# The same attention and MLP kernel with its instructions put in another order: lengths in the planner changed, ranks of runs of operations shifted

## The chip, the core and the metric

The kernel runs on one core of a Trainium2 chip. The metric is device time in microseconds, the median of several executions. The engines are TensorE (PE, matmuls; its weight loads are shown as PEld), VectorE (DVE), ScalarE (ACT), GpSimd (POOL) and SyncE (SP, which here issues DMAs). Each takes its own instructions strictly in the order in which they were written.

## The reference

A chunk-selecting attention over 4 batches, 8 heads, 768 tokens, 64 dimensions, and then an MLP over all 3072 tokens (512 to 2048 to 512, with ELU):

```python
k_min = np.min(k_chunks, axis=3)
k_max = np.max(k_chunks, axis=3)
ub = np.sum(np.maximum(q * k_min, q * k_max), axis=-1)
ub = np.where(causal, ub, -1000000000.0)
top_chunks = np.argsort(ub, axis=-1)[..., -top_k:]
scores = scale * np.matmul(q, k.transpose(0, 1, 3, 2))
mask = sel & (pos[:, None] >= pos[None, :])
...
attn = attn / (np.sum(attn, axis=-1, keepdims=True) + 1e-09)
return np.matmul(attn, v).astype(np.float32)
...
h = x @ w_in
g = np.where(h > 0.0, h, alpha * (np.exp(np.minimum(h, 0.0)) - 1.0))
return (g @ w_out).astype(np.float32)
```

Keys come in 24 chunks of 32. For each query and chunk an upper bound of the score is computed from the chunk's smallest and largest key values; the 6 best causal chunks are kept. Scores outside them and above the diagonal are masked.

## The kernel before

**Tiling.** Two heads make a pair, so a batch has 4 pairs and the whole problem 16. A pair's 768 queries are done in two halves of 384. Two pairs make a quad, for which chunk selection is done together. The MLP is done for a batch's half (384 tokens) at a time.

**The stages of a pair.** Loads of q, k and v (`stage`, `vd`; L396, L437; in the first batch `gT`, L475, L481), issued by SP. In batch 0 (`first_prep`) fp32 matmuls turn q and k (L498), ACT copies k in bf16 with a strided pattern (L508), POOL casts q (L548) and v (L539). In the other batches (`pair_prep`) DVE transposes k and q (L409, L427) and reduces k's chunks to minimum and maximum (L413), and POOL casts two heads of k, two of q, and v (L548, L440). `quad_sel` computes the chunk bounds (PE, L580), their six best (DVE, L597 to L620), and puts the mask rows into `rhs` (POOL, L631). `pair_attend` does scores (PE, L672), exponentials (ACT, L699), the diagonal (POOL, L718), the product with values (PE, L731), the division (DVE, L744, L747), and a transpose to `xT` (PE L756, ACT L759).

**The MLP.** `mlp` computes 16 up projections of 4 matmuls (L781) into `psH` (into `psS` in the last batch), the exponential (ACT, L791), the rest of ELU into `gT` (ACT L796, DVE L799, or DVE L820 and L825; L809 and L814 in the last batch), and for each of 3 token tiles 4 parts of 4 down projections (L838) into `psM` (`psMT` in the last batch), evicted by ACT (L846) and stored by SP (L850). An MLP operation can run as soon as its batch's `xT` is there, so the MLP of one batch is interleaved with the attention of the next.

**The order.** Nothing is emitted directly. Every step is registered with `add(engine, length, rank, emit, ...)` in a planner (`Plan`), with what it reads, writes, and which buffers it takes and frees. `Plan.order` then plays the engines through: repeatedly it takes, for each engine, the operation that can start first by the planned lengths; among those ready when the engine is free, the one with the lowest rank `prio` goes first. The engine whose choice starts earliest is served. Operations are emitted in this sequence, and that is the order of each engine's instructions on the chip. The ranks are positions in units of one pair: `pos(u, hf)` for attention, `mpos(b, hf)` for the MLP, less a lead for loads and preparation. Lengths are formulas, `act(n)` for ACT, `dve(n)` for DVE, and for POOL casts `0.13 + 0.00096 * n`. The plan treats POOL and those DVE operations marked `port` as exclusive of each other.

Of the kernel before, what the change touches and what calls it, by code (L numbers as in the profile page):

```python
# [17 lines left out]
S = 768  # L18
# [10 lines left out]
HALF = S // 2  # L29
# [22 lines left out]
LATER = {4: 0}  # L52
RATES = (232.0, 232.0, -1.4, 0.75)
MERGE = (False, False, False, True)

DUMP = None

# [6 lines left out]
class Plan:  # L64
# [17 lines left out]
    def add(self, eng, dur, prio, emit, reads=(), writes=(), alloc=(), free=(), lat=None, tag="",  # L82
# [33 lines left out]
        self.ops.append(o)  # L116
        return o

    def order(self):
        ops = self.ops  # L120
        for o in ops:
            o.left = len(o.deps) + len(o.after)
            o.ready = 0.0
            o.start = o.end = None
            for d in o.deps:
                d.users.append(o)
            for d in o.after:
                d.followers.append(o)
        free_slots = {c: [(0.0, i) for i in range(n)] for c, n in self.caps.items()}
        held = {}  # L130
        engines = {}
        waiting = {}
        for o in ops:
            waiting.setdefault(o.eng, [])
            engines[o.eng] = self.BEGIN
            if not o.left:
                waiting[o.eng].append(o)
        n_left = len(ops)
        port = {"POOL": 0.0, "DVE": 0.0}
        out = []  # L140
        while n_left:
            best = None
            for e, t in engines.items():
                cand = None
                for o in waiting[e]:
                    r = max(t, o.ready)
                    if o.port and o.eng in port:
                        r = max(r, port["DVE" if o.eng == "POOL" else "POOL"])
                    ok = True
                    for h in o.alloc:  # L150
                        fs = free_slots[h[0]]
                        if not fs:
                            ok = False
                            break
                        r = max(r, min(fs)[0])
                    if not ok:
                        continue
                    key = (r, o.prio, o.n) if r > t else (t, o.prio, o.n)
                    if cand is None or key < cand[0]:
                        cand = (key, o, r)  # L160
                if cand is not None and (best is None or cand[2] < best[2]):
                    best = cand
            assert best is not None, "no operation can start"
            _, o, r = best
            slots = []
            for h in o.alloc:
                fs = free_slots[h[0]]
                s = min(x for x in fs if x[0] <= r)
                fs.remove(s)
                held[h] = s[1]  # L170
                slots.append((h, s[1]))
            o.start = r
            o.end = r + o.dur
            engines[o.eng] = o.end
            if o.port and o.eng in port:
                port[o.eng] = o.end
            waiting[o.eng].remove(o)
            for h in o.free:
                free_slots[h[0]].append((o.end + o.lat, held[h]))
            for u in o.users:  # L180
                u.left -= 1
                lag = 0.0 if u.eng == o.eng and o.eng in ("PE",) else o.lat
                u.ready = max(u.ready, o.end + lag)
                if not u.left:
                    waiting[u.eng].append(u)
            for u in o.followers:
                u.left -= 1
                u.ready = max(u.ready, o.start)
                if not u.left:
                    waiting[u.eng].append(u)  # L190
            out.append((o, slots))
            n_left -= 1
        return out
# [3 lines left out]
def kernel(  # L197
# [88 lines left out]
    add = plan.add  # L286
# [99 lines left out]
    def pair_prep(u):  # L386

        kb, qb, vx, km = new("kb", "qb", "vx", "km")
        PAIR[u] = dict(kb=kb, qb=qb, vx=vx, km=km)

        def load(h, src):
            def f():
                for hd in range(2):
                    for e in range(2):
                        r0 = 64 * hd + 32 * e
                        nc.sync.dma_start(out=tiles[h][r0:r0 + 32, :].rearrange("c (m i) -> c m i", i=32),  # L396
                                          in_=src[2 * u + hd, e])
            return f

        kd, qd, kt, qt, qa, kx, vd = new("stage", "stage", "kt", "qt", "qa", "kx", "vd")  # L400
        pa = pos(u, 0)
        pl = pa - 4.0
        pr = pa - AHEAD
        for i in range(2):
            PAIR[u]["qt", i], PAIR[u]["qa", i] = qt, qa
        late = [("asked", LATER[u])] if u in LATER else []
        fetch(2.0, 393.0, 128.0, pl, load(kd, ke), [kd], alloc=[kd], reads=late)
        fetch(2.0, 393.0, 128.0, pl + 0.2, load(qd, qe), [qd], alloc=[qd], reads=late)
        add("DVE", dve(S), pr, lambda: nc.vector.transpose(out=tiles[kt], in_=tiles[kd]),  # L409
            reads=[kd], writes=[kt], alloc=[kt], free=[kd])  # L410
        for x, op in ((0, AOT.min), (1, AOT.max)):
            add("DVE", dve(S), pr,
                lambda x=x, op=op: nc.vector.tensor_reduce(  # L413
                    out=tiles[kx] if x else tiles[km][:, 0, 0:NCH],
                    in_=tiles[kt].rearrange("p (c w) -> p c w", w=CHUNK),
                    axis=mybir.AxisListType.X, op=op),
                reads=[kt, "kept"], writes=[kx] if x else [(km, 0, i) for i in range(2)],
                alloc=[kx] if x else [km])
        add("POOL", 0.16, pr,
            lambda: nc.gpsimd.tensor_tensor(out=tiles[km][:, 1, 0:NCH], in0=tiles[kx], in1=tiles[km][:, 0, 0:NCH],  # L420
                                            op=AOT.subtract),
            reads=[kx] + [(km, 0, i) for i in range(2)], writes=[(km, 1, i) for i in range(2)], free=[kx])
        for hd in range(2):
            cast(pr + 0.2, S, lambda hd=hd: (tiles[kb][0:64, hd, :], tiles[kt][64 * hd:64 * hd + 64, :]),
                 reads=[kt], writes=[(kb, i, hd) for i in range(2)], alloc=[] if hd else [kb],
                 free=[kt] if hd else [])
        add("DVE", dve(S), pr + 0.1, lambda: nc.vector.transpose(out=tiles[qt], in_=tiles[qd]),  # L427
            reads=[qd], writes=[qt], alloc=[qt], free=[qd])
        add("ACT", act(S - SEL0), pr + 0.1,
            lambda: nc.scalar.activation(out=tiles[qa], in_=tiles[qt][:, SEL0:S], func=AF.Relu),  # L430
            reads=[qt], writes=[qa], alloc=[qa])
        for hd in range(2):
            cast(pr + 0.2, S, lambda hd=hd: (tiles[qb][0:64, hd, :], tiles[qt][64 * hd:64 * hd + 64, :]),
                 reads=[qt], writes=[(qb, i, hd) for i in range(2)], alloc=[] if hd else [qb])

        def vload():
            nc.sync.dma_start(out=tiles[vd], in_=v3[:, 12 * u:12 * u + 12, :])  # L437
        fetch(0.5, 393.0, 205.0, pl + 1.2, vload, [vd], alloc=[vd], reads=late)
        add("POOL", 0.13 + 0.00096 * S, pr + 1.0,
            lambda: nc.gpsimd.tensor_copy(out=tiles[vx][:, :, 0:D], in_=tiles[vd]),  # L440
            reads=[vd, "ones"], writes=[(vx, i) for i in range(2)], alloc=[vx], free=[vd])

    def first_prep(u, hf):
# [60 lines left out]
            return x.rearrange("q (j p) -> q p j", j=4)  # L504
        add("PE", TURN, pr, turn(bk, at_k), reads=[(hk, i0), "ident"], writes=[bk[0]], alloc=bk, free=fk)
        for hd in range(2):
            add("ACT", act(HALF), pr,
                lambda hd=hd: nc.scalar.activation(  # L508
                    out=tiles[kb][0:64, hd, a:b].rearrange("q (p j) -> q p j", j=4),
                    in_=tok(ps(bk, None, None)[64 * hd:64 * hd + 64, :]), func=AF.Copy),  # L510
                reads=[bk[0]], writes=[(kb, hf, hd), (bk[0], "turn")], alloc=[] if hf or hd else [kb])
# [23 lines left out]
        for hd in range(2):  # L535
            cast(pr + 0.2, HALF, lambda hd=hd: (tiles[qb][0:64, hd, a:b], tiles[qt][64 * hd:64 * hd + 64, a:b]),
                 reads=[qt], writes=[(qb, hf, hd)], alloc=[] if hf or hd else [qb])
        add("POOL", 0.13 + 0.00096 * HALF, pr + 1.0,
            lambda: nc.gpsimd.tensor_copy(  # L539
                out=tiles[vx].rearrange("p (h n) d -> p h n d", h=2)[:, :, 3 * hf:3 * hf + 3, 0:D],  # L540
                in_=tiles[sv][:, iv].rearrange("p (h n d) -> p h n d", h=2, d=D)),
# [3 lines left out]
    def cast(pr, w, what, **kw):  # L545
        def f():
            o, i = what()
            nc.gpsimd.tensor_copy(out=o, in_=i)  # L548
        add("POOL", 0.13 + 0.00096 * w, pr, f, **kw)

    def quad_sel(g, hf):

# [210 lines left out]
    def mlp(b, hf):  # L763
        tail = b == B - 1
        if True:
# [64 lines left out]
            for tt in range(3):  # L830
                bm = bank("MT" if tail else "M")
                for part in range(4):
                    pr = mpos(b, hf) + 2 + 2 * (4 * tt + part) / 12

                    def down(bm=bm, tt=tt, part=part, gt=gt):
# [2 lines left out]
                            nc.tensor.matmul(pm, lhsT=tiles[gt][:, fc, 128 * tt:128 * tt + 128],  # L838
                                             rhs=w_out_sb[:, fc, :], start=(fc == 0), stop=(fc == NFC - 1))
                    add("PE", 4 * 0.2165, pr, down,  # L840
                        reads=[("w_out", part)] + [(gt, fc) for fc in range(4 * part, 4 * part + 4)],
                        writes=[(bm[0], part)], alloc=bm if part == 0 else [],
                        free=[gt] if tt == 2 and part == 3 else [])
                osb, = new("osb")
# [92 lines left out]
```

## Time and profile before

| what | value |
|---|---|
| median of 3 runs | 280.38 us (280.21 to 285.49) |
| span of the profiled execution, first to last instruction | 278.4 us |
| median less span | 2.0 us |
| bytes moved by DMA | 29.82 MB |
| DVE, ACT, POOL busy | 73%, 72%, 46% of the span |

A time for the profiled execution that includes what lies around its span is not given; the median of the runs stands in for it. Busy time of PE includes each matmul's pipeline latency up to its modelled end, so a busy PE is not PE at its peak. In groups, the first number after the bar is busy time in us, the next the mean of one instruction in ns, and after the second bar stands idle time of the engine ahead of those instructions with what ended it. In the waits, the three numbers are the total in us, the number of waits, and the longest. The chain of waits follows the work that ended last back to what released it; in order of time its rows have start, length and what ran.

### The profile page before, as it was taken

The page shows a single profiled execution, that of the slowest core. Times are in us where ns is not written, and L with a number is a line of the kernel's source. Part 1 is how long each engine was busy: PE and PEld are TensorE (multiplying, and loading weights), DVE is VectorE, ACT ScalarE, POOL GpSimd, SP SyncE. Part 2 cuts the span into 40 slices and gives each one's busy share as a digit, 9 for nine tenths or more (in the row PEclk, how much of TensorE's full clock was granted, in tenths as well). Part 3 has the DMA queues.
Part 4 walks back from the last instruction along what each step waited for, and adds up shares of the span by engine and source line. Part 5 has one row for each costly group of instructions (what it writes and reads, how often), then busy time and mean ns, then how long its engine had stood idle before and what let it go on. Part 6 is the DMA issues. An engine that isn't in the chain of part 4 may idle for free.

```text
span 278.4 us, 7242 instructions
## 1 busy us (share of the span) xinstructions
PE 266.7 (96%) x2732; PEld 164.0 (59%) x2732; DVE 204.2 (73%) x546; ACT 201.4 (72%) x381; POOL 128.0 (46%) x235
## 2 busy tenths in 40 slices
PE   7989899989999999999999999999999999999994
PEld 7968566644565556655665656565565556555541
DVE  6876965799999989999989588657856434767610
ACT  2879899946699697999899958685868564544311
POOL 5668863356797797966965625102320201000000
PEclk9999999999999999999999999999999999999999
DMA  7999999988998599999497101101101111101122
GB/s 187 232 211 188 197 203 207 146 131 163 189 171 156 73 143 201 165 163 170 87 164 114 38 2 38 40 0 40 39 4 38 40 39 40 38 0 40 38 75 75
DMA packets 111330, 29.82 MB, mean 107 GB/s; under 512 B 101056, under 2 KB 108224, under 8 KB 111296
## 3 DMA queue, kind: packets, MB, share of 16 engines
q1 hardware_dynamic: 106656, 24.78, 48.4%
q0 software_dynamic: 4224, 4.19, 9.2%
q8 instruction: 21, 0.34, 0.6%
q10 hardware_dynamic: 416, 0.39, 0.5%
q14 instruction: 13, 0.11, 0.1%
HBM read 27.26 MB, written 6.29 MB: 121 GB/s over the span
## 4 chain that ended last, share of the span: by engine, by line
PE 68%; ACT 15%; DVE 6%; DMA 4%; issue 3%; SPq 1%; POOL 0%; ACTq 0%; DVEq 0%
PE psM L838 20%; PE psH L781 15%; PE psS L781 7%; PE psMT L838 7%; PE psS L672 7%; ACT pt L699 7%; PE psO L731 5%; ACT e L791 3%; PE psS L580 3%; DMA gT<-in_v_dram 2%; DMA gT<-in_k_dram 2%; ACT psH L796 1%; ACT xT L759 1%; DVE gT L799 1%; PE psT L756 1%
## 5 line engine op out<-in xcount | busy, mean ns | idle before, releaser
L699 ACT ACTIVATE pt<-psS 128x768 bf16<-128x768 f32 (+1 forms) x120 | 91.5, 799 | 4.1 <-PE psS L672 2.6
L781 PE MATMUL psH<-xT,w_in_sb 128*128 128x384 bf16 x384 | 75.2, 325 | 1.6 <-ACT xT L759 0.9
L838 PE MATMUL psM<-w_out_sb,gT 128*128 128x512 bf16 x288 | 72.5, 379 | 0.4 <-DVE gT L825 0.2
L781 PEld LDWEIGHTS <-w_in_sb 128*128 128x128 bf16 x512 | 47.6, 97 | 34.8 <-issue 4.0
L791 ACT ACTIVATE e<-psH 128x384 f32<-128x384 f32 x96 | 48.3, 519 | 22.4 <-PE psH L781 21.9
L838 PEld LDWEIGHTS <-gT 128*128 128x128 bf16 x384 | 36.2, 98 | 35.0 <-DVE gT L825 0.6
L718 POOL TENSOR_SCALAR_AFFINE_SELECT pt<-pt 128x256 bf16<-128x256 bf16 (+1 forms) x56 | 29.0, 519 | 56.7 <-ACT pt L699 55.7
L672 PE MATMUL psS<-rhs,lhs 88*128 88x384 bf16 (+4 forms) x304 | 51.5, 283 | 1.6 <-ACT pt L699 0.9
L672 PEld LDWEIGHTS <-lhs 88*128 88x128 bf16 x304 | 27.8, 97 | 15.8 <-issue 1.5
L631 POOL COPY rhs<-selt 24x192 bf16<-24x192 bf16 (+2 forms) x56 | 25.5, 456 | 21.9 <-DVE selt L620 18.6
L799 DVE SCALAR_TENSOR_TENSOR gT<-e,psH 128x384 bf16<-128x384 f32 x48 | 25.6, 539 | 13.3 <-ACT psH L796 13.2
L731 PEld LDWEIGHTS <-pt 128*128 128x128 bf16 x672 | 27.8, 98 | 11.3 <-issue 3.8
L548 POOL CAST rhs<-qt 64x768 bf16<-64x768 f32 (+1 forms) x40 | 28.5, 711 | 12.3 <-ACT qt L526 6.1
L820 DVE SCALAR_TENSOR_TENSOR t<-e,psH 128x384 bf16<-128x384 f32 x48 | 25.9, 543 | 9.6 <-ACT e L791 9.2
L731 PE MATMUL psO<-vext,pt 128*128 128x65 bf16 x672 | 30.2, 194 | 1.7 <-DVE gT L799 1.1
L791 ACT ACTIVATE e<-psS 128x768 f32<-128x768 f32 x16 | 13.0, 810 | 19.0 <-PE psS L781 19.0
L825 DVE SCALAR_TENSOR_TENSOR gT<-psH,t 128x384 bf16<-128x384 f32 x48 | 25.9, 543 | 0.8
L796 ACT ACTIVATE psH<-psH 128x384 f32<-128x384 f32 x48 | 25.1, 528 | 0.0
L781 PE MATMUL psS<-xT,w_in_sb 128*128 128x384 bf16 x128 | 23.2, 326 | 0.0
L548 POOL CAST lhs<-kt 64x768 bf16<-64x768 f32 x24 | 19.6, 819 | 6.8 <-DVE kt L409 3.7
L838 PE MATMUL psMT<-w_out_sb,gT 128*128 128x512 bf16 x96 | 22.5, 379 | 0.0
L759 ACT ACTIVATE xT<-psT 128x384 bf16<-128x384 bf16 x32 | 16.5, 515 | 4.5 <-PE psT L756 4.4
(66 smaller groups left out, 293.4 us busy)
## 6 DMA issues: line engine op xcount, KB each, us to landing
out_dram<-osb SPq DMA_DIRECT2D x24, 256.0 KB, 2.0
vd<-in_v_dram SPq DMA_DIRECT2D x12, 384.0 KB, 5.2
stage<-in_k_dram SPq DMA_DIRECT2D x48, 96.0 KB, 3.4
stage<-in_q_dram SPq DMA_DIRECT2D x48, 96.0 KB, 3.6
w_in_sb<-in_moe_w_in_dram POOLq DMA_DIRECT2D x4, 512.0 KB, 11.5
w_out_sb<-in_moe_w_out_dram POOLq DMA_DIRECT2D x4, 512.0 KB, 8.8
gT<-in_v_dram SPq DMA_DIRECT2D x16, 96.0 KB, 4.3
gT<-in_k_dram SPq DMA_DIRECT2D x6, 192.0 KB, 5.5
```

What stands on the lines that cost most here:

```text
L548: nc.gpsimd.tensor_copy(out=o, in_=i)
L672: nc.tensor.matmul(p_s[:, hd, pc:pc + w], lhsT=tiles[pt_["kb"]][0:64 + NCH, hd, 128 * kb:128 * kb + 128], rhs=tiles[pt_["qb"]][0:64 + NCH, ...
L699: lambda bs=bs, pt=pt, wtot=wtot, lo=lo, at=at: nc.scalar.activation(out=tiles[pt][:, :, lo:lo + wtot], in_=tiles[bs[0]][:, :, at:at + wto ...
L718: nc.gpsimd.affine_select(out=a, in_=a, compare_op=AOT.is_ge, fill=0.0, base=0, pattern=pat, channel_multiplier=-1)
L731: nc.tensor.matmul(po[:, hd, qi, :], lhsT=tiles[pt][:, hd, off:off + 128], rhs=tiles[pt_["vx"]][:, 6 * hd + kb, :], start=(kb == 0), stop= ...
L781: nc.tensor.matmul(ph, lhsT=w_in_sb[:, kk, f0:f0 + 128], rhs=tiles[XT[4 * b + kk]][:, c0:c0 + HALF], start=(kk == 0), stop=(kk == NKK - 1))
L791: lambda e=e, view=view: nc.scalar.activation(out=tiles[e][:, 0:step], in_=view(), func=AF.Exp),
L796: lambda view=view: nc.scalar.activation(out=view(), in_=view(), func=AF.Relu),
L799: lambda e=e, view=view, fc=fc, gt=gt: nc.vector.scalar_tensor_tensor(out=tiles[gt][:, fc:fc + step, :], in0=tiles[e][:, 0:step], scalar=1 ...
L820: lambda e=e, t=t, view=view: nc.vector.scalar_tensor_tensor(out=tiles[t][:, 0:step], in0=tiles[e][:, 0:step], scalar=1.0, in1=view(), op0 ...
L825: lambda t=t, view=view, fc=fc, gt=gt: nc.vector.scalar_tensor_tensor(out=tiles[gt][:, fc:fc + step, :], in0=view(), scalar=0.0, in1=tiles ...
L838: nc.tensor.matmul(pm, lhsT=tiles[gt][:, fc, 128 * tt:128 * tt + 128], rhs=w_out_sb[:, fc, :], start=(fc == 0), stop=(fc == NFC - 1))
```

## The change

It does three things, all in the planner's input. No instruction is added or removed.

1. The planned length of POOL's casts is 0.13 + 0.00084n instead of 0.13 + 0.00096n; that of ACT's strided copy of k in the first batch is 0.495 instead of `act(384)`.
2. Each part of a down projection now depends on the part before it.
3. Ahead of `order`, `shift` adds to the ranks. For each of 83 fixed numbers a small generator is drawn: either the whole list is cut into runs of 5 to 64 operations and each run's ranks move by a common amount (one of the 83), or one window of 1 to 80 operations does (the other 82), in about half of them only the operations of one engine.

```diff
+SHIFTS = (264975, 480031, 781933, 78890, 970076, 386297, 51472, 476552, 906048, 761004, 513050, 307835, 837141, 857068,
...
+    def shift(self, seeds):
+        ops = self.ops
+        n = len(ops)
+        for seed in seeds:
+            x = [seed]
+
+            def draw():
+                x[0] = (6364136223846793005 * x[0] + 1442695040888963407) % 2 ** 64
+                return (x[0] >> 40) / 16777216.0
+            draw(), draw()
+            if draw() < 0.1:
+                amp = draw() * 0.8
+                j = 0
+                while j < n:
+                    w = 5 + int(draw() * 60)
+                    m = amp * (draw() - 0.5) * 2
+                    for o in ops[j:j + w]:
+                        o.prio += m
+                    j += w
+            else:
+                a = int(draw() * n)
+                v = draw()
+                w = 1 + int(v * v * v * 80)
+                amp = draw()
+                amp = 0.1 + 2.4 * amp * amp
+                m = amp * (draw() - 0.5) * 2
+                one = draw() < 0.5
+                for o in ops[a:a + w]:
+                    if not one or o.eng == ops[a].eng:
+                        o.prio += m
+
     def order(self):
         ops = self.ops
+        self.shift(SHIFTS)
...
-        add("POOL", 0.13 + 0.00096 * S, pr + 1.0,
+        add("POOL", 0.13 + 0.00084 * S, pr + 1.0,
...
-            add("ACT", act(HALF), pr,
+            add("ACT", 0.495, pr,
                 lambda hd=hd: nc.scalar.activation(
...
-        add("POOL", 0.13 + 0.00096 * HALF, pr + 1.0,
+        add("POOL", 0.13 + 0.00084 * HALF, pr + 1.0,
...
-        add("POOL", 0.13 + 0.00096 * w, pr, f, **kw)
+        add("POOL", 0.13 + 0.00084 * w, pr, f, **kw)
...
                     add("PE", 4 * 0.2165, pr, down,
-                        reads=[("w_out", part)] + [(gt, fc) for fc in range(4 * part, 4 * part + 4)],
+                        reads=[("w_out", part)] + [(gt, fc) for fc in range(4 * part, 4 * part + 4)]
+                        + ([(bm[0], part - 1)] if part else []),
                         writes=[(bm[0], part)], alloc=bm if part == 0 else [],
```

6 rows, old and new, of the table SHIFTS are left out of this document.

## The prediction

> **What bounds the kernel now.** I read the page first, then the windows, the chain of waits in order of time, and the groups by shape.
>
> ```profile
> span 278.4 us, 7242 instructions
> PE 266.7 (96%) x2732; PEld 164.0 (59%) x2732; DVE 204.2 (73%) x546; ACT 201.4 (72%) x381; POOL 128.0 (46%) x235
> PEclk9999999999999999999999999999999999999999
> ...
> PE 68%; ACT 15%; DVE 6%; DMA 4%; issue 3%; SPq 1%; POOL 0%; ACTq 0%; DVEq 0%
> ```
>
> TensorE is busy 96% of the span at full granted clock, and no other engine is over 73%. Yet the chain gives PE only 68%: for a third of the span something else decided when the next matmul could start. The windows say when:
>
> ```profile
> 0.00:30.00 30.00, 27.00 (x507) 24.01 (x509) 21.73 (x85) 21.78 (x50) 20.77 (x52) 1.00 1.03 204
> 30.00:60.00 30.00, 27.34 (x299) 16.97 (x294) 22.33 (x59) 26.98 (x52) 16.25 (x29) 1.00 1.18 181
> 60.00:140.00 80.00, 77.77 (x870) 46.04 (x869) 76.38 (x221) 66.41 (x128) 62.27 (x107) 1.00 0.90 152
> 140.00:270.00 130.00, 130.00 (x1046) 75.17 (x1044) 83.80 (x184) 85.08 (x151) 28.68 (x49) 1.00 0.18 43
> 270.00:278.40 8.40, 4.54 (x22) 1.86 (x19) 0.00 (x0) 1.19 (x2) 0.00 (x0) 1.00 0.17 62
> ```
>
> After the length come PE, PEld, DVE, ACT and POOL. From 140 to 270 us PE has no hole at all (130.00 of 130). In the last stretch it stops 3.86 us before the end (8.40 less 4.54): the last eviction and store, which no order shortens. The holes of the first three stretches are 3.00, 2.66 and 2.23 us, 7.9 together. That is a lower bound, because a matmul's modelled end covers the start of a hole.
>
> The better measure is the time that the same matmuls take back to back. The steps come from dense pieces of the chain, the counts from the groups:
>
> ```profile
> 254.66 1.30 PE psS L781 x8
> ...
> 263.32 11.24 PE psMT L838 x52
> ...
> 91.53 0.71 PE psO L731 x22
> ...
> 66.72 0.81 PE psS L580 x32
> ...
> 19.96 0.81 PE psH L498 x16
> ```
>
> ```profile
> L781 PE MATMUL psH<-xT,w_in_sb 128*128 128x384 bf16 x384 | 75.2, 325 | 1.6 <-ACT xT L759 0.9 <-DVE gT L799 0.2 <-DVE gT L825 0.2
> L838 PE MATMUL psM<-w_out_sb,gT 128*128 128x512 bf16 x288 | 72.5, 379 | 0.4 <-DVE gT L825 0.2
> L781 PE MATMUL psS<-xT,w_in_sb 128*128 128x384 bf16 x128 | 23.2, 326 | 0.0
> L838 PE MATMUL psMT<-w_out_sb,gT 128*128 128x512 bf16 x96 | 22.5, 379 | 0.0
> L672 PE MATMUL psS<-rhs,lhs 88*128 88x384 bf16 x152 | 34.0, 325 | 0.6 <-ACT pt L699 0.4
> L731 PE MATMUL psO<-vext,pt 128*128 128x65 bf16 x672 | 30.2, 194 | 1.7 <-DVE gT L799 1.1 <-DVE gT L825 0.4
> L756 PE MATMUL psT<-ident_b,on 128*128 128x128 bf16 x96 | 10.7, 220 | 0.3
> ```
>
> Up projection: 512 x 1.30/8 = 83.2. Down projection: 384 x 11.24/52 = 83.0. Scores: 152 at the 384-wide step of 0.1625 are 24.7; the kernel issues another 152 narrower ones, which I put at half that, 12.4. Values: 672 x 0.71/22 = 21.7. Output transposes: 96 at a third of 0.1625, 5.2. Chunk bounds: 14 groups of 32 at 0.81 each, 11.3. First-batch turns: 16 groups of 16 at 0.81, 13.0. The diagonal masks and 28 warm-up matmuls: about 4.8, an estimate. The sum is 259.3. The span is 19.1 longer. Of that 3.9 is the end, and about 1.1 lies ahead of the warm-up matmuls. **About 14 us remain for which PE starves, nearly all before 140 us.** This is all that an order can win: the floor is 278.4 - 14 = 264 of span. The median of the runs is 280.38, 2.0 above this span, so I add 2.0: no time below 266.
>
> What such starvation looks like, in the chain and in the timeline of PE:
>
> ```profile
> 31.71 0.97 PE psH L781 x5
> ...
> 38.74 1.42 ACT pt L699 x2
> ...
> 53.80 0.98 DVE kt L409
> ...
> 55.67 0.95 DVE kx L413
> ...
> 56.99 0.97 DVE qt L427
> ```
>
> ```profile
> 57.13 1.11 PE L731 MATMUL psO<-vext,pt 128*128 128x65 bf16 x30 [0.84 <-DVE gT L799]
> ```
>
> Around 38 us exponentials set the pace. From 53.8 us DVE does the next batch's transposes and reductions, about 1 us each, while the activations of the first MLP (gT) wait behind them; PE then stands for 0.84 us. Both are questions of what an engine takes first, and ranks decide that.
>
> **The change, part by part.** The instructions stay: same matmuls, copies, loads. Computing the order costs nothing on the chip. Three edits alter what the planner sees.
>
> Lengths. POOL casts are planned at 0.13 + 0.00084n in place of 0.13 + 0.00096n, and the strided k copies at 0.495 in place of 0.062 + 0.00082 x 384 = 0.377.
>
> ```profile
> 83.85 0.82 POOL L548 CAST lhs<-kt 64x768 bf16<-64x768 f32 x1
> 84.61 0.83 POOL L548 CAST rhs<-qt 64x768 bf16<-64x768 f32 x1
> ```
>
> ```profile
> 29.09 0.98 ACT L508 ACTIVATE lhs<-psH 64x384 bf16<-64x384 f32 x2
> ```
>
> Consecutive casts of 768 start 0.76 apart; the old plan said 0.867, the new says 0.775. Twelve pairs have five such casts, so the old plan had 60 x 0.107 = 6.4 us of POOL work that did not exist, and the new one has 0.9. The k copies take 0.49 each: 16 were planned 0.113 too short, 1.8 us in sum, now right. On PE's path this is worth nothing directly. Indirectly a truer plan puts scores behind casts where they really end; bounds 0 to 2 us, I take 1, since the casts' error is spread over 60 instructions on an engine that is 46% busy.
>
> The half-width casts are less clear:
>
> ```profile
> 10.31 0.93 DVE L337 COPY lhs<-econ 32x768 bf16<-32x768 bf16 x2
> 10.32 1.28 POOL L548 CAST rhs<-qt 64x384 bf16<-64x384 f32 x2 [1.09 <-ACT qt L526]
> ...
> 11.67 0.50 POOL L539 CAST vext<-gT 128x384 bf16<-128x384 f32 x1
> ```
>
> Two casts of 384 beside two DVE copies took 1.28, or 0.64 each, while one without that neighbour took 0.50. The new length is 0.453, so here it is farther off than the old 0.499. The Trainium skill (GPSIMD Engine Reference, section 8, Key points) says that POOL shares its SBUF interfaces with VectorE and contends with DVE instructions in a two-port mode; the trace agrees, with 0.64 against 0.50. By it, moved operations meet such neighbours in new places. That is a rival below.
>
> The order of the four parts of a down projection is now a dependency. The plan has no lag between two PE operations, and all four read parts of one gT, filled in that order. Cost nothing, hidden by other PE work; if that cover is gone, a late chunk holds the three parts behind it, 4 x 0.2162 = 0.86 each, but they would wait for the last chunk anyway.
>
> Ranks. Working the diff's draw rule through its numbers: one of the 83 shifts every run of operations by up to 0.29; 82 shift one window each, 37 of them on a single engine. The windows have a median of 8 operations and a median shift of 0.27, 13 reach 1 or more, and 61 of 82 begin in the first 65% of the list. One rank unit is one of 16 pairs of heads. So most are small nudges in the parts where PE starves, not in the tail that is dense already. They move loads on SP, prep on DVE and POOL, exponentials on ACT and matmuls on PE; what is moved ahead on an in-order queue holds all behind it.
>
> What can come of it: of the visible 7.9 us of holes, 1.1 is the start and 1.9 the rest of the first 30 us, where turns wait for loads. The share behind 30 us is 4.9 of 6.8, 72%; of the 14 us that is about 10. Bounds for an order that mends it: 0 and 10. I take six tenths, 6.0, because the dense stretch behind 140 us shows that with enough ready work PE has no hole, and that MLP work is there from 32 us on; four tenths I leave to ACT, which has only 30.00 - 26.98 = 3.0 us free in the second stretch. Together with a small part of the lengths' 1 us (0.2, since both mend the same holes): 278.4 - 6.2 = 272.2 of span, **274.2 us**. What is late next is ACT between 30 and 60 us.
>
> **The rivals.**
>
> Wash. PE's hole closes in one place and opens in the next, since ACT, at 26.98 of 30, and DVE, at 76.38 of 80, have nearly no room. For it: those two rows. Against it: DVE's work in 60 to 140 is partly the next batch's prep and could lie later, when DVE has 46 us free. Time: 278 to 283, say 280.4.
>
> Longer casts where POOL meets DVE. All 16 half-width casts of q last 0.64 where the plan has 0.453: 3.0 us of POOL in the first 30 us, where selection, scores and so MLP start behind it. Added to the forecast, 277.2. Against it: POOL's own waits, the next rows, show that it usually waits for others.
>
> ```profile
> POOL pt L718 <- ACT pt L699: 55.7, 28, 9.9
> ...
> DVE kt L409 <- DMA stage<-in_k_dram: 0.2, 1, 0.2
> ```
>
> Slower: a load behind a store. SP issues loads and output stores in order. A store waits in the queue until its eviction is done:
>
> ```profile
> SPq L850 <- ACT osb L846: 121.1, 17, 10.8
> ```
>
> ```profile
> stage<-in_k_dram SPq DMA_DIRECT2D x48, 96.0 KB, 3.4
> ```
>
> If a shifted rank puts a pair's k or q load behind such a store, the load leaves up to 10.8 us late, and DVE's transpose, casts and scores of that pair follow. Today loads are early enough that DVE waits 0.2 us in all; how early, no row says. With slack of two landings (2 x 3.4, an estimate) it costs 4.0; with one, 10.8 - 3.4 = 7.4. It decides when the slack is under 5.2 us. I price it at 7.4: 287.8. A plan made tight by search has less slack than this one, which speaks for it; that the plan charges a store's wait to SP speaks against it.
>
> That the change does nothing (ranks only break ties, so the order stays): 280.4, but windows of 40 to 75 operations shifted by more than 1 rank cannot all be idle. It counts within the wash.
>
> **How the numbers follow.** Chances: forecast 0.56, wash 0.20, longer casts 0.06, slower 0.18. The forecast itself lies between 270 (holes mended to ten tenths, 280.4 - 10) and 277; four in five of its chance is below 274.8. So faster by over 2% (below 274.8; 2% is about what a measurement of this kernel can tell from no change) has 0.45. Slower by over 2% (above 286.0) has 0.18: the queue's price range of 4.0 to 7.4 and beyond reaches 284 to 290, and a few such in a row count with it. Within 2% is the rest, 0.37. Range: 270 to 285.5, which leaves out some 0.04 below and 0.15 above. The likeliest case by itself is 270 to 277.
>
> **What would show it.** Right: PE busy sum unchanged near 266 but the first two stretches shorter; the fully dense stretch begins earlier than 140 us; the MLP's first down projections come sooner; chain share of PE over 70%. The lengths' part shows in casts that end before PE asks for them. Wash: same dense start, other names in the waits of PE. Casts: L548 of 64x384 above 0.60 on the mean and first exponentials of the MLP later than 32 us. Slower: DVE waiting for DMA on kt or qt by several us, a store ahead of loads in SP's timeline, and a drop in the busy share of PE between 60 and 140 us. The forecast is wrong if the holes before 140 us are set by loads and ACT's sum alone, so that no rank reaches them.

## The result, and the profile after

The changed kernel takes 292.19 us (median of 4, 290.34 to 293.98), the kernel before beside it 280.94 (median of 4). The ratio is 1.0396, 95% interval 1.0322 to 1.0470: slower by 4%, where 274.2 us and a gain of 2% had been forecast. Some executions of several kernels here take about 4 us longer at a lower granted clock; the medians keep them, the ratios leave them out. The profiled execution of the changed kernel took 290.34 us at a span of 288.6.

From the page of the changed kernel, the busy totals, then the slices of PE, DVE and the granted clock, and the chain:

```profile
span 288.6 us, 7249 instructions
...
PE 264.8 (92%) x2732; PEld 162.1 (56%) x2732; DVE 202.8 (70%) x546; ACT 202.5 (70%) x381; POOL 128.0 (44%) x235
...
PE   8888980499979999999999999999999999999994
...
DVE  7956940667999799899999746997647527575620
...
PEclk9999996599999999999999999999999999999998
...
PE 68%; DMA 9%; DVE 8%; ACT 6%; SPq 3%; issue 3%; POOL 2%; ACTq 0%; DVEq 0%; POOLq 0%
```

The work is the same (PE 264.8 against 266.7 us, DVE 202.8 against 204.2). What is new is one place, slices 7 and 8 of 40: in the seventh PE and DVE fall to nothing, and the granted clock falls to six and then five tenths. In the chain DMA has gone from 4% to 9%. The windows, with the columns as before the change, show where the span grew:

```profile
0.00:30.00 30.00, 25.54 (x513) 22.01 (x514) 20.90 (x75) 22.15 (x51) 20.69 (x53) 1.00 1.08 214
30.00:60.00 30.00, 17.33 (x170) 10.53 (x170) 15.85 (x55) 16.94 (x32) 11.83 (x21) 0.77 1.07 166
60.00:140.00 80.00, 77.18 (x892) 46.65 (x890) 71.71 (x201) 67.62 (x129) 56.84 (x96) 1.00 0.81 137
140.00:270.00 130.00, 130.00 (x1090) 76.05 (x1089) 90.51 (x213) 91.74 (x165) 38.65 (x65) 1.00 0.23 50
```

From 30 to 60 us PE is busy 17.33 us where it had been 27.34: 10.0 us are gone in that stretch alone, against 1.5 in the stretch before it (25.54 against 27.00) and 0.6 in the one behind (77.18 against 77.77). The waits of the changed kernel (total, times, longest) name the end of the chain:

```profile
DVE kt L449 <- DMA stage<-in_k_dram: 12.4, 1, 12.4
PE psH L821 <- DVE gT L839: 11.8, 1, 11.8
```

Each is a single wait. Before the change DVE waited 0.2 us in all for k loads. The timeline of SP, DVE and PE around it (start, length, and in brackets the idle time ahead):

```profile
25.77 12.23 SPq L436 DMA_DIRECT2D stage<-in_q_dram  x4
38.10 14.45 SPq L436 DMA_DIRECT2D stage<-in_k_dram  x8
...
53.04 0.98 DVE L449 STREAM_TRANSPOSE kt<-stage 128x768 f32<-128x768 f32 x1 [12.37 <-DMA stage<-in_k_dram]
53.95 0.52 DVE L839 SCALAR_TENSOR_TENSOR gT<-e,psH 128x384 bf16<-128x384 f32 x1
...
54.51 1.44 PE L821 MATMUL psH<-xT,w_in_sb 128*128 128x384 bf16 x4 [11.77 <-DVE gT L839]
```

It reads like this. SP loads the fifth pair's q first and its k second (the row of eight holds the sixth pair's k as well). DVE's next instruction is the transpose of that k, and DVE stands 12.37 us ahead of it. Behind it in DVE's queue is the ELU step that would free a bank of `psH`; PE's next up projection needs that bank and stands 11.77 us. ACT and POOL run dry too (11.88 and 10.70 us). Nothing in the MLP work depends on k: it waits because DVE takes its instructions in order.

The same part of SP's queue in the kernel before:

```profile
24.62 16.61 SPq L396 DMA_DIRECT2D stage<-in_k_dram  x4
41.33 10.33 SPq L396 DMA_DIRECT2D stage<-in_q_dram  x4
```

There k went first, and DVE came to it at 53.80 us (the prediction's chain has that row), 12.6 us after SP was through with issuing it (24.62 + 16.61 = 41.23).

Why an order like this was made is to be read from the planner. The loads have two operations each: the issue on SP, and the transfer on an engine called "DMA", which exists only in the plan and serves one transfer at a time, by rank. The kernel's own `order` gives, for the fifth pair (planned us):

```
                       issue of k   issue of q   transfer of k   kt on DVE
before                       22.0         24.0            46.1        51.2
changed                      23.9         21.9            33.9        39.0
```

Before the change the weights' transfers fill the plan's DMA without a gap up to 46.1 us, and k comes behind them. In the changed plan there is a gap at 33.9, k's transfer is put into it, and kt is planned 12.2 us earlier. The gap is 0.05 us wide: the plan's DMA is free at 33.93, and the fifth weights' transfer is asked for at 33.98, where the plan before had asked for it at 33.06. That q's issue goes ahead of k's comes from a single one of the 83 draws. Its window is 13 operations long, begins with k's transfer and moves them by -1.19; so it takes k's transfer, q's issue and kt forward and leaves k's issue, the operation just ahead of the window, where it was. With that one draw left out, the planner issues k first again, and still plans kt at 39.0.

The planner's own forecast for the whole change is a gain of 1.7 us: its order ends at 271.0 us, against 272.7 before.

On the chip nothing puts a transfer into the gap: the two queues run at once.

```profile
q0 software_dynamic: 3012, 2.99, 61.5%
q1 hardware_dynamic: 13961, 1.93, 45.3%
```

These are the DMA queues of the changed kernel from 30 to 60 us (packets, MB, share): the weights' queue and that of SP's loads. Their shares come to 106.8% of the same 30 us, so the two overlap, where the plan has one transfer after the other. The Trainium skill (DMA: Bandwidth & Descriptors, section Queues, rings and completion order) says that an engine goes round its queues packet by packet; the trace agrees, with 61.5% and 45.3% in the same 30 us.

### The profile page after: what moved, and what is told of

Same layout as the page of the kernel before. It is cut to its first block, busy times and chain, and to the rows that moved or that the text cites. A ratio compares the mean times of both kernels' runs of the same rounds, so it can differ in the third digit from the quotient of the medians.

```text
span 288.6 us, 7249 instructions
## 1 busy us (share of the span) xinstructions
PE 264.8 (92%) x2732; PEld 162.1 (56%) x2732; DVE 202.8 (70%) x546; ACT 202.5 (70%) x381; POOL 128.0 (44%) x235
## 4 chain that ended last, share of the span: by engine, by line
PE 68%; DMA 9%; DVE 8%; ACT 6%; SPq 3%; issue 3%; POOL 2%; ACTq 0%; DVEq 0%; POOLq 0%
PE psM L878 20%; PE psH L821 14%; PE psS L712 9%; PE psS L821 7%; PE psMT L878 7%; PE psO L771 6%; DMA stage<-in_k_dram 4%; ACT pt L739 3%; DMA gT<-in_k_dram 2%; SPq L436 2%; DMA gT<-in_q_dram 2%; DVE thr L649 2%; PE psT L796 2%; DVE kt L449 1%; PE psS L620 1%
## 5 line engine op out<-in xcount | busy, mean ns | idle before, releaser
L739 ACT ACTIVATE pt<-psS 128x768 bf16<-128x768 f32 (+3 forms) x120 | 91.6, 793 | 8.4 <-PE psS L712 7.1
L821 PE MATMUL psH<-xT,w_in_sb 128*128 128x384 bf16 x384 | 75.4, 328 | 12.1 <-DVE gT L839 11.8
L821 PEld LDWEIGHTS <-w_in_sb 128*128 128x128 bf16 x512 | 47.9, 98 | 48.0 <-issue 14.1
L831 ACT ACTIVATE e<-psH 128x384 f32<-128x384 f32 x96 | 47.6, 513 | 27.9 <-PE psH L821 25.1
L712 PE MATMUL psS<-rhs,lhs 88*128 88x384 bf16 (+4 forms) x304 | 52.9, 286 | 4.0 <-POOL rhs L671 2.5
L758 POOL TENSOR_SCALAR_AFFINE_SELECT pt<-pt 128x256 bf16<-128x256 bf16 (+1 forms) x56 | 29.7, 532 | 59.2 <-ACT pt L739 57.7
L588 POOL CAST rhs<-qt 64x768 bf16<-64x768 f32 (+1 forms) x40 | 27.7, 693 | 10.4 <-ACT qt L566 6.4
L771 PEld LDWEIGHTS <-pt 128*128 128x128 bf16 x672 | 26.7, 98 | 7.0 <-DVE on L787 0.6
L771 PE MATMUL psO<-vext,pt 128*128 128x65 bf16 x672 | 29.3, 195 | 0.4
L849 DVE TENSOR_SCALAR t<-e 128x768 bf16<-128x768 f32 x16 | 9.0, 560 | 16.4 <-ACT e L831 16.4
```

Source lines behind the costliest of these rows:

```text
L712: nc.tensor.matmul(p_s[:, hd, pc:pc + w], lhsT=tiles[pt_["kb"]][0:64 + NCH, hd, 128 * kb:128 * kb + 128], rhs=tiles[pt_["qb"]][0:64 + NCH, ...
L739: lambda bs=bs, pt=pt, wtot=wtot, lo=lo, at=at: nc.scalar.activation(out=tiles[pt][:, :, lo:lo + wtot], in_=tiles[bs[0]][:, :, at:at + wto ...
L758: nc.gpsimd.affine_select(out=a, in_=a, compare_op=AOT.is_ge, fill=0.0, base=0, pattern=pat, channel_multiplier=-1)
L771: nc.tensor.matmul(po[:, hd, qi, :], lhsT=tiles[pt][:, hd, off:off + 128], rhs=tiles[pt_["vx"]][:, 6 * hd + kb, :], start=(kb == 0), stop= ...
L821: nc.tensor.matmul(ph, lhsT=w_in_sb[:, kk, f0:f0 + 128], rhs=tiles[XT[4 * b + kk]][:, c0:c0 + HALF], start=(kk == 0), stop=(kk == NKK - 1))
L831: lambda e=e, view=view: nc.scalar.activation(out=tiles[e][:, 0:step], in_=view(), func=AF.Exp),
```

## The experiments

Theory A: a load that the plan has too early, with its first user early in DVE's queue, makes the whole loss. Rival B: the shifted order is worse as a whole. Rival C: the changed lengths do it. Rival D: k is needed then anyway, so a later kt only moves the hole. Ratios are to the kernel before in the same job.

**The two loads exchanged in the changed kernel.** Applied to the finished order:

```diff
+    at = [next(i for i, (o, _) in enumerate(steps) if o.n == n) for n in (527, 529)]
+    a, b = min(at), max(at)
+    x, y = steps[a][1][0][1], steps[b][1][0][1]
+    steps[a], steps[b] = (steps[b][0], steps[b][1]), (steps[a][0], steps[a][1])
+    other = {x: y, y: x}
+    for i in range(a, len(steps)):
+        o, slots = steps[i]
+        steps[i] = (o, [(h, other.get(s, s) if h[0] == "stage" else s) for h, s in slots])
```

> The changed kernel with two neighbours in SP's queue exchanged: the fifth pair's k load goes ahead of its q load, as before the change; the buffers of the two are exchanged with them, and nothing else moves. Theory A (q ahead of k makes k land near 53 us, DVE stands at kt for 12.4 us, PE's psum banks are not freed, PE stands 11.8 us and its clock halves): k lands near 41 to 44 us, DVE's wait for k is under 4 us, the clock is 1.00 all through, the time is 276 to 281. Rival B (the whole order is worse, this hole is only where the loss shows): the hole moves or stays above 8 us, time 287 to 293. Rival C (the planned lengths are to blame): no change from the changed kernel's 292.

Measured: 285.95 us, ratio 1.0208 (1.0144 to 1.0272). Its timeline:

```profile
25.08 14.99 SPq L436 DMA_DIRECT2D stage<-in_k_dram  x4
...
47.88 0.98 DVE L449 STREAM_TRANSPOSE kt<-stage 128x768 f32<-128x768 f32 x1 [5.85 <-DMA stage<-in_k_dram]
...
49.34 1.44 PE L821 MATMUL psH<-xT,w_in_sb 128*128 128x384 bf16 x4 [5.24 <-DVE gT L839]
```

The hole shrinks by 6.5 us, from 11.77 to 5.24, and the ratio by 0.0188 (1.0396 - 1.0208), 5.3 us of 280.9: the hole and the time move together, against rivals B and C. But the expectations of under 4 us of waiting and of 276 to 281 us were too good. SP was done issuing k at 40.07, and it landed only at 47.9. About half the loss comes with q ahead of k; the other half stays with a place for kt that is too early even so.

**The same exchange, the other way, in the kernel before.** The same lines there.

> The kernel before with the same two loads exchanged the other way: q of the fifth pair ahead of its k, buffers exchanged with them. Here DVE's transpose of k stands late in DVE's order (it ran at 53.8 us). Theory A (two conditions are needed: k late and kt early in DVE's order): k lands near 52 us, DVE waits under 3 us, time 280 to 284. If q ahead of k alone is the price: a hole of 8 us or more, time 288 to 293.

Measured: 282.34 us, ratio 1.0039 (0.9991 to 1.0088). With q first, kt ran without a wait of its own:

```profile
54.02 0.97 DVE L409 STREAM_TRANSPOSE kt<-stage 128x768 f32<-128x768 f32 x1
```

So a late k by itself costs nothing that is clear of noise (the interval allows 0.9%), as long as DVE comes to it late. An early kt with k first was not tried in this kernel; in the changed kernel it is the run above, with a hole of 5.24 us.

**Only kt and what hangs on it later.** In the changed kernel, with q still ahead of k:

```diff
+    group = {531, 532, 533, 534, 535, 536, 546}
+    moved = [x for x in steps if x[0].n in group]
+    steps = [x for x in steps if x[0].n not in group]
+    i = next(i for i, (o, _) in enumerate(steps) if o.eng == "DVE" and o.start >= 52.0)
+    steps[i:i] = moved
```

> The changed kernel with seven of its 1707 operations emitted later and nothing else moved: the fifth pair's kt on DVE, its two reductions, the difference and two casts on POOL, and the q load that takes kt's staging buffer go from planned 39.0 us to planned 52.0 us. q is still loaded ahead of k. Theory A (kt stands in DVE's queue before its data is there): DVE's wait for k under 2 us, no hole of PE over 2 us at 42 to 54 us, clock 1.00, time 274 to 280. Rival B (the order as a whole is worse): 284 or more with the loss spread over other holes. Rival D (k and its casts are needed at 54 us, so a later kt only moves the hole to the scores of the next batch): a hole of 5 us or more at 60 to 80 us, 284 to 290.

Measured: 280.83 us, ratio 0.9972 (0.9928 to 1.0015). Seven of 1707 operations take back the whole 4%; the time lies just above the range expected (274 to 280). kt ran without a wait of its own:

```profile
53.85 0.98 DVE L449 STREAM_TRANSPOSE kt<-stage 128x768 f32<-128x768 f32 x1
```

Page and windows of this kernel:

```profile
PEclk9999999999999999999999999999999999999999
```

```profile
0.00:30.00 30.00, 26.43 (x510) 22.88 (x512) 21.07 (x75) 22.30 (x51) 20.42 (x53) 1.00 1.07 210
30.00:60.00 30.00, 27.02 (x292) 16.87 (x288) 22.81 (x70) 26.36 (x50) 15.59 (x28) 1.00 1.18 175
60.00:140.00 80.00, 76.92 (x868) 46.12 (x875) 76.28 (x219) 67.19 (x128) 60.98 (x104) 1.00 0.89 152
```

The clock is whole, and PE is busy 27.02 of the second 30 us, nearly as before the change (27.34); 27 of its matmul records are missing in this trace, which can only lower these numbers. Rivals B and D fall: the rest of the shifted order is as good as the old one. It is not much better either: the lower bound of the interval allows a gain of 0.7%. Its longest hole is one that the kernel before does not have, where scores wait for POOL's mask rows:

```profile
72.09 0.81 PE L712 MATMUL psS<-rhs,lhs 88*128 88x384 bf16 x6 [1.90 <-POOL rhs L671]
```

**Both mendings:** k first, and the group at planned 47.5 us.

> Both mendings: k ahead of q in SP's queue, and the same seven operations emitted at planned 47.5 us, since k landed at 47.9 us with k first. Theory A: DVE's wait for k under 2 us, time 274 to 280, and no better than the later kt alone by more than 2 us. Rival D: a hole at 60 to 80 us, 284 or more.

Measured: 279.14 us, ratio 0.9948 (0.9903 to 0.9994). This is the best version found, about half a per cent faster than the kernel before, with the interval just clear of no change.

**The fault put into the kernel before.** q ahead of k as above, and one DVE instruction moved:

```diff
+    moved = [x for x in steps if x[0].n == 531]
+    steps = [x for x in steps if x[0].n != 531]
+    i = next(i for i, (o, _) in enumerate(steps) if o.eng == "DVE" and o.start >= 39.0)
+    steps[i:i] = moved
```

> The kernel before with the two faults put in by hand: q of the fifth pair ahead of its k in SP's queue, and one DVE instruction, the transpose that makes kt, emitted at planned 39 us instead of 51.2 us. No length, no rank and no other order differs from the kernel before. Theory A: DVE stands 10 to 14 us at kt, PE 8 to 12 us, clock near 0.5 behind it, time 288 to 294, the loss of the changed kernel. Rival B (the loss is of the order as a whole): under 284.

Measured: 290.73 us, the median of four that lie far apart (284.85 to 296.27), beside 283.0 for the kernel before; no ratio is given. The waits of its slowest execution, longer than expected:

```profile
DVE kt L409 <- DMA stage<-in_k_dram: 17.3, 2, 15.4
...
PE psH L781 <- DVE gT L799: 14.3, 2, 14.1
```

The hole appears in the old order, with the old lengths and without a shift, from one transpose and one exchange of loads. Its size in the time is less sure than the hole itself, for the four runs spread by 11 us.

**The parts of the change alone.** Without the shifts (the line `self.shift(SHIFTS)` left out):

> The changed kernel without the shifts: the new lengths and the order of down-projection parts alone. Theory A: the fifth pair's kt is planned behind the weight transfers as before, no hole at 42 to 54 us, time 279 to 285. Rival C (the lengths are to blame): 287 or more, with a hole at kt.

Measured: 289.13 us (284.62 to 290.19), ratio 1.0241 (1.0118 to 1.0365). Slower than expected, by how much is uncertain, for the ratio rests on two executions, 284.62 and 288.87. It is not by the hole at kt, which is planned at 51.5 us here. The planned end of this order is 276.8 us against 272.7 before the change: by the planner's own reckoning, its choice in order of rank came out 4 us worse with the new lengths and the order of parts. What on the chip makes the loss stays open.

With the shifts and the old lengths:

```diff
-        add("POOL", 0.13 + 0.00084 * w, pr, f, **kw)
+        add("POOL", 0.13 + 0.00096 * w, pr, f, **kw)
...
-            add("ACT", 0.495, pr,
+            add("ACT", act(HALF), pr,
```

> The changed kernel with the old lengths of POOL casts and of ACT's k copies: the shifts and the order of parts alone. q still goes ahead of k and kt still stands early in DVE's order. Theory A: a hole of 10 to 17 us at kt, clock 0.5 behind it, time 288 to 297. Rival C: no hole, 278 to 284.

Measured: 297.09 us, ratio 1.0614 (1.0545 to 1.0683). In the waits of PE a hole is there in this one too, now ahead of another matmul, behind the same kind of DVE stall:

```profile
DVE kt L449 <- DMA stage<-in_k_dram: 10.3, 1, 10.3
...
PE psO L771 <- DVE on L787: 12.0, 2, 11.6
```

The old lengths do not take the hole away; lengths are not what makes the hole; as its cause, rival C falls. Why the time is longer than with the new lengths was not followed; in the plan too this order ends later, at 277.2 us against 271.0.

**The planner mended, for the fifth pair.**

```diff
-        add("DMA", size / rate, pr, lambda: None, reads=[w], writes=writes, lat=2.0)
+        behind = [("asked", 7)] if kw.get("reads") else []
+        add("DMA", size / rate, pr, lambda: None, reads=[w] + behind, writes=writes, lat=2.0)
```

> The changed kernel with one line of the planner mended: the transfers of the fifth pair's k and q are planned behind all eight weight transfers, as the kernel before had them by its ranks, so that a shifted rank cannot bring them forward. All shifts and new lengths stay; the order is planned anew, with kt near 54 us. Theory A: no hole of PE over 2 us at 42 to 54 us, DVE's wait for k under 1 us, clock 1.00, time 278 to 282. Rival B (shifted ranks are harmful in themselves): 285 or more.

Measured: 296.71 us, ratio 1.0562 (1.0521 to 1.0602), worse than the change itself. Its timeline says why:

```profile
57.09 0.98 DVE L450 STREAM_TRANSPOSE kt<-stage 128x768 f32<-128x768 f32 x1 [14.87 <-DMA stage<-in_k_dram]
```

This kt is the sixth pair's. With the fifth pair's transfer held back, the planner put the sixth pair's k into the same gap at 33.9 us, and its kt at 39.0 us in DVE's order. The forecast for this kernel was wrong (278 to 282); the mechanism is the same, one load further on: PE stands 14.26 us behind that kt.

**The planner mended for all pairs.** The same lines with `behind = [("asked", 7)] if pr >= 0.0 and rate < 200.0 else []`.

> The changed kernel with the planner's transfers of q and k of every pair behind the first batch planned after all eight weight transfers, not those of the fifth pair alone, where the sixth pair's k took the place that the fifth had left and DVE stood 14.9 us for it. Shifts and new lengths stay; the first kt is planned at 53.2 us. Theory A: no wait of DVE for a k load over 2 us, no hole of PE over 2 us at 40 to 60 us, clock 1.00, time 279 to 284. Rival B (shifted ranks are harmful in themselves): 285 or more with the loss in other holes.

Measured: 283.73 us, ratio 1.0050 (1.0001 to 1.0100). With all shifts and all new lengths, and only these transfers planned behind the weights', 3.5 of the 4 per cent are gone; DVE's wait for k is 0.6 us.

**The hole filled with matmuls of zeros.** Ahead of the matmul that stands:

```diff
+            if o.n == 399:
+                fill = psum.tile([P, 2, 512], F32, name="fill", tag="two0")
+                for _ in range(46):
+                    nc.tensor.matmul(fill[:, 0, :], lhsT=blank, rhs=w_in_sb[:, 0, 0:512], start=True, stop=True)
```

> The changed kernel with 46 matmuls of zeros (128 x 512, about 10 us at the dense step of 0.216) put on PE just ahead of the matmul that stands 11.8 us, into a psum bank that is free then. They compute nothing that is used; the hole keeps its cause and its length. If the halved clock behind the hole has a price of its own, the clock is 1.00 at 46 to 60 us and the time falls by 1.5 to 4 us below the changed kernel's, to 288 to 290.5. If the clock costs nothing because DVE and ACT set the pace behind the hole: 291 to 293 with the clock at 1.00.

Measured: 293.13 us, ratio 1.0449 (1.0408 to 1.0491), no faster than the changed kernel. The timeline of PE and three windows of it:

```profile
44.27 10.09 PE L948 MATMUL fill<-w_in_sb,blank 128*128 128x512 bf16 x46
55.91 0.81 PE L821 MATMUL psH<-xT,w_in_sb 128*128 128x384 bf16 x4 [1.55 <-DVE gT L839]
```

```profile
48.00:52.00 4.00, 4.00 (x20) 1.80 (x19) 0.00 (x0) 0.00 (x0) 0.00 (x0) 1.00 1.26 193
52.00:56.00 4.00, 2.45 (x12) 1.06 (x11) 1.56 (x3) 0.00 (x0) 0.51 (x1) 1.00 0.88 109
56.00:60.00 4.00, 2.92 (x31) 2.07 (x31) 3.97 (x8) 2.67 (x6) 1.99 (x4) 0.76 0.61 98
```

The clock stays at 1.00 through the hole, but falls to 0.76 just behind it, in 56 to 60 us. So neither expectation was met as written: the filler only put the low clock off, and what it costs over the whole run stays open. For the first matmuls behind the hole the traces show it. The changed kernel, at a clock of 0.50 there:

```profile
54.51 1.44 PE L821 MATMUL psH<-xT,w_in_sb 128*128 128x384 bf16 x4 [11.77 <-DVE gT L839]
55.75 1.48 PE L712 MATMUL psS<-rhs,lhs 88*128 88x384 bf16 x4
57.03 0.64 PE L771 MATMUL psO<-vext,pt 128*128 128x65 bf16 x8
```

The filled kernel, behind the up projection at 55.91:

```profile
56.56 0.81 PE L712 MATMUL psS<-rhs,lhs 88*128 88x384 bf16 x4
58.33 0.60 PE L771 MATMUL psO<-vext,pt 128*128 128x65 bf16 x8 [0.95 <-DVE on L787]
```

The eight matmuls are nearly twice as fast, but then PE stands 0.95 us for DVE: from the first up projection to the product with values it is 2.52 us in the changed kernel and 2.42 in the filled one. The mended kernel bounds the rest: without hole and low clock the ratio is 0.9972, so both together are 0.0424 of 280.9, 11.9 us, give or take some 2 us by the intervals, and the hole alone is 11.8 us in the trace. That leaves little for the clock.

## Why the prediction was wrong

**What bounds the kernel.** Right in kind: about 14 us of starving ahead of 140 us, a dense stretch behind. In the changed kernel the dense stretch holds the same (130.00 of 130), and most of the loss lies in 30 to 60 us.

**The term of the ranks is the step that failed.** It was put at a gain of 6.0 us with bounds of 0 and 10, on the ground that an order can fill the holes since MLP work is there. It measured as a loss: 1.0396 with the hole, and at best 0.9948 with both faults mended, about 1.5 us. Three things were wrong in it. The bounds left out a loss, although the prediction named ahead of it that what is moved ahead on an in-order queue holds all behind it: a transpose moved ahead of its late k held DVE for 12.4 us and PE for 11.8. The six tenths were a share of PE's holes on the chip, while the planner, which alone turns ranks into an order, forecast 1.7 us. And the four tenths left to ACT were far too few: with the hole gone PE is busy 26.43, 27.02 and 76.92 us in the first three stretches, where it had been 27.00, 27.34 and 77.77 before, so the other holes are about as large as they were, which is what the rival called the wash had said (278 to 283).

**What the ranks moved was not looked at by name.** The diff's numbers could tell sizes and places in the list, and the prediction stopped there. That the shifted windows also hold operations of the plan's own "DMA" engine, whose order no instruction carries out, was to be read from `fetch`, and was missed. So was the one window that splits a load: it holds k's transfer and not k's issue.

**The slower rival** had the right family and the right sign to look for (DVE waiting for DMA on kt by several us; it waited 12.4), and its price of 7.4 us was too low. It had the wrong cause: k was late behind a q load, in a stretch in which the weights came in, and not behind a store, and k's slack was lost at both ends, by a later landing and an earlier transpose. The exchange alone, which is the nearest to that rival, costs nothing clear of noise in the kernel before (1.0039). Of the signs named for it one came, DVE's wait on kt; no store went ahead of the loads, and PE's busy share fell between 30 and 60 us and hardly between 60 and 140.

**The lengths** were costed at a gain of 0 to 2 us. Together with the order of parts, and without the shifts, they made the time 2.4% longer (1.0118 to 1.0365, from two executions). That they are nearer to the trace was right for the wide casts, and did not help there: the greedy choice answered to them with another order, which ends 4 us later in the plan itself.

**The contention of half-width casts** was not tried by itself; its sign, a mean above 0.60 us, did not come (0.50 in the changed kernel, 0.55 before). The order of the down projection's parts at nothing was not tried by itself either; the mended kernels carry it and lose nothing by it that shows.

**The range** (270 to 285.5) left out the slower rival even at its own price, 287.8, and the 292.19 measured lies beyond the 284 to 290 named for that rival too: no single stall of 12 us was among the prices.

## What to carry to other kernels

When an order is searched with a planner, ask first which of its engines are real. A gain that comes from re-ranking something that no instruction controls, here the order in which transfers share the DMA engines, is a gain in the plan alone, and it turns into a stall where an in-order engine trusts the landing time. Before the whole order is judged, look for the first user of each late load and what stands behind it in that engine's queue: moving seven operations was worth 4% here. And where a planner makes the order, play it through and read its own forecast first: here it promised 1.7 us, and it showed a load whose first user had moved 12 us ahead.

## What was not expected of the hardware

While the weights come in, SP itself is slow to issue. In the changed kernel, from 24 to 56 us, the issues of q and k loads on SP took (min, median, max, in ns):

```profile
L436 SPq DMA_DIRECT2D stage<-in_q_dram x8: 312/669/6505, 25.8 to 55.5; - x8
L436 SPq DMA_DIRECT2D stage<-in_k_dram x8: 525/1804/3419, 38.1 to 52.0; - x8
...
DMA to landing us min/median/max: 2.4/7.0/13.1
```

One issue took up to 6.5 us and a landing up to 13.1, while the shortest took 0.3 and 2.4. A load on SP's queue so delays not only its own data but the issue of every load behind it; the planner has 2.0 us for four issues, and the four of q took 12.23. The kernel before has the same: from 0.3 to 6.8 us for one issue of k between 24.6 and 59.5 us. Why an issue takes so long is not shown.

The clock fell to 0.76 in the filled kernel (56 to 60 us) although the matmul that had stood 11.8 us stood only 1.55 us there, behind 10 us of dense matmuls of zeros. Which of the short holes around it brought that about (1.55 and 0.95 us) is not shown.
